# A first weight block fetched by two queues, weight conversions moved half a piece ahead, and two masks moved from DVE to ScalarE and GpSimd

## The chip, the cores and the metric

One core of a Trainium2 chip runs the kernel. The metric is the device time in microseconds of one execution. Engines are named as the profile names them: PE is TensorE, DVE VectorE, ACT ScalarE, POOL GpSimd, SP SyncE (here only an issuer of transfers); a q behind a name is the engine's instruction queue.

## What is computed

A gated linear attention over 768 steps for 4 batches and 8 heads of 48, and a feed-forward block on its output:

```python
for t in range(S):                       # S = 768, D = 48
    state = alpha[t][:, None] * state + outer(k[t], v[t])
    y[t] = q[t] @ state
x = y as (tokens 3072, 384)
h = x @ w_in                             # 384 x 1024
solu = h * softmax(h)
ln = (solu - mean) / sqrt(var + 1e-6) * g_ln
out = ln @ w_out                         # 1024 x 384
```

The weights w_in and w_out arrive as 64-bit floats, and the kernel turns them into 32-bit ones on the chip.

## The kernel before, in words

The 768 steps are cut into G = 6 groups of 128; one group holds 128 steps of all 4 batches, 512 tokens. Within a group the recurrence is done as matmuls: scaled keys and queries (running products of alpha, the scans of L220), scores of 128 x 128 per batch and head, a mask that keeps the causal half (`masked`, L290), then `read_values` (L343), which multiplies the masked scores with v and copies the result to x on ACT (L351). `keys_back` (L298) and `next_state` (L353) bring the state to the next group.

The feed-forward block then goes over the 1024 hidden columns in eight blocks f of 128. `up_mm` (L385) computes h for block f on PE: three matmuls, which stand as six records in the trace. `up_act` (L395) lets ACT make e = Exp(h) (L403), DVE the product u = h * e (L404) and ACT its Square (L405). `down` (L494) multiplies u with w_out. h has two banks in PSUM.

The order of the work is written out by hand, engine by engine, in program order: each engine executes its instructions in the order in which the code names them, and there is no scheduler that moves them. The group 0 part, L645 to L745, is the part that the change touches. It is also where the weights come in:

- `pieces` (L543) are eight: 0 to 3 are 256 columns each of w_in, 4 to 7 are 256 rows each of w_out.
- `fetch(i, slot, n)` (L552) issues on SP the transfers of n pieces from piece i on into raw space. For w_in that is 16 transfers: eight of 32 rows (4 KB a row, 128 KB) and eight of 16 rows (64 KB). `fetch(0, 3, 2)` (L662) brings pieces 0 and 1, `fetch(2, 1, 2)` (L663) pieces 2 and 3. Ahead of them SP issues alpha, k, q and v of group 0. In front of each transfer the issuing engine waits for the earlier transfer that used the same of eight semaphores.
- `bits(i, half)` (L585) converts a piece on DVE in five instructions: two in half 0 (L595, L598), three in half 1 (L603, L606, L607). `in_range(i)` (L575) lets ACT look for values out of range (L582, L583).
- `scaled` (L609) multiplies w_out rows with g_ln on ACT.

In the attention part of group 0, scores are in eight tiles: four (`a`, heads 0 to 3 of each batch) and four (`a_h`, `a_h`, `a_o`, `a_o`, heads 4 to 7 of batches 0 to 3). DVE masks all eight (L293). In the loop over f at L713 DVE does the product of f and then half a piece of conversion, `bits(2 + f // 2, f % 2)`, so that the four pieces 2 to 5 are spread over eight steps; bits(6) and bits(7) follow behind the loop. The loop also holds ACT work at fixed steps: in_range(2) at f = 1, copies of the ends of k and q at 2 and 3, in_range(3) at 3, in_range(4) at 5, scaled at 6 and 7.

Of the kernel before, what the change touches and what calls it, by code (L numbers as in the profile page):

```python
# [11 lines left out]
U32 = mybir.dt.uint32  # L12
I32 = mybir.dt.int32
AF = mybir.ActivationFunctionType
ALU = mybir.AluOpType
AX = mybir.AxisListType
P = 128
# [15 lines left out]
def fast_path(ctx, tc, q, k, v, alpha, moe_w_in, moe_w_out, moe_g_ln, out):  # L33
# [12 lines left out]
    nc = tc.nc  # L46
    B, H, S, D = q.shape
# [4 lines left out]
    NP = H // 2  # L52
# [26 lines left out]
    mask = const.tile([P, P], FP, name="mask")  # L79
    ones = const.tile([P, P], FP, name="ones")  # L80
# [8 lines left out]
    mean_sb = const.tile([P, DM], FP, name="mean_sb")  # L89
# [11 lines left out]
    qn = const.tile([P, H, TQ, D], FP, name="qn")  # L101
# [29 lines left out]
    sT = const.tile([P, B, H, P], FP, name="sT")  # L131
# [13 lines left out]
    def by_token(x):  # L145

        return x.rearrange("p h u d -> p (h u d)").rearrange("p (b h d) -> p b h d", b=B, h=H)

    def load_first(src, dst, g):
        t = slice(g * P, (g + 1) * P)  # L150
        for b in range(0, B, 2):
            nc.sync.dma_start(
                out=by_token(dst)[:, b : b + 2].rearrange("p b h d -> p (b h) d"),
                in_=src[b : b + 2, :, t].rearrange("b h p d -> p (b h) d"),
            )

    def ends_of(src, tag=None):

        ends = ring.tile([P, T4], FP, name=tag) if tag else two.tile([P, T4], FP, tag="two", name="ends")
        ends = ends.rearrange("p (b d) -> p b d", b=B)  # L160
        nc.scalar.copy(out=ends.rearrange("p b (h d) -> p b h d", h=H), in_=by_token(src)[:, :, :, E0:D])
        return ends
# [83 lines left out]
    def apart():  # L246
        for i in range(2):
            nc.scalar.mul(
                out=qv[:, H : 2 * H].rearrange("p (j i) t -> p j i t", i=2)[:, :, i], in_=qe, mul=parity[:, i : i + 1]
            )  # L250
# [19 lines left out]
    def quarter(b):  # L270
        return slice(32 * b, 32 * b + 32)

    def banks(name, shape, n=B):
        return [ps_a.tile([P] + shape, FP, tag=f"a{b}", name=f"{name}{b}") for b in range(n)]

    def scores(g, half, a=None):
        a = a or banks("a", [NP, P])
        for i in range(NP):
            h = half * NP + i
            for kb, qb in ((h, h), (H + h // 2, H + h)):  # L280
                for b in range(B):
                    nc.tensor.matmul(  # L282
                        a[b][:, i], lhsT=kT[quarter(b), kb], rhs=qv[quarter(b), qb], start=kb == h, stop=kb != h,
                        tile_position=(32 * b, 0), skip_group_check=True,
                    )
        masks[half] = a
# [3 lines left out]
    def masked(half, batches=range(B)):  # L290
        a = masks[half]
        for b in batches:
            nc.vector.tensor_tensor(  # L293
                out=sT[:, b, half * NP : half * NP + NP], in0=a[b], in1=mask[:, None, :].to_broadcast([P, NP, P]),
                op=ALU.mult,
            )
# [11 lines left out]
    parts = [(a, [(NP * a + r, first_of[r % 2]) for r in range(NP)]) for a in range(2)]  # L308
# [237 lines left out]
    def place(i):  # L546
        kind, f = pieces[i]
        return w_out[:, f : f + 2, 0:DM] if kind else w_in[:, :, f * P : f * P + 2 * P]

    raws = {}  # L550

    def fetch(i, slot, n=1):  # L552

        kind, f = pieces[i]
        w = n * F // (2 if kind else KC)
        raw = room[:, 1536 * slot : 1536 * (slot + n)].bitcast(U32).rearrange("p (c f w) -> p c f w", f=w, w=2)
        if kind:
            parts = [(slice(0, P), c, moe_w_out[(f + c) * P : (f + c + 1) * P, :]) for c in range(2)]
        else:
            rows = moe_w_in[:, f * P : f * P + w].rearrange("(h d) f -> h d f", d=D)  # L560
            parts = [(slice(E0 * r, E0 * r + E0), c, rows[NP * c + r, 0:E0]) for c in range(2) for r in range(NP)]
            parts += [(slice(E1 * h, E1 * h + E1), 2, rows[h, E0:D]) for h in range(H)]
        for rows, c, src in parts:
            if float64:
                nc.sync.dma_start(out=raw[rows, c].rearrange("p f w -> p (f w)"), in_=src.bitcast(U32))
            else:
                dst = w_out[rows, f + c, 0:DM] if kind else w_in[rows, c, f * P : f * P + w]
                nc.sync.dma_start(out=dst, in_=src)
        for m in range(n):
            raws[i + m] = raw[:, :, w // n * m : w // n * (m + 1)]  # L570

# [13 lines left out]
    def bits(i, part=None):  # L585
        if not float64:
            return
        lo, hi = raws[i][:, :, :, 0], raws[i][:, :, :, 1]
        if part != 1:
            made[i] = [  # L590
                two.tile([P, F], FP, tag="two", name=x).rearrange("p (c f) -> p c f", c=hi.shape[1])
                for x in ("top", "low")
            ]
            top = made[i][0].bitcast(U32)
            nc.vector.tensor_scalar(  # L595
                out=top, in0=hi, scalar1=3, scalar2=0x3FFFFFF8, op0=ALU.logical_shift_left, op1=ALU.bitwise_and
            )
            nc.vector.scalar_tensor_tensor(  # L598
                out=top, in0=hi, scalar=0xC0000000, in1=top, op0=ALU.bitwise_and, op1=ALU.bitwise_or
            )  # L600
        if part != 0:
            top, low = made.pop(i)
            nc.vector.tensor_scalar(  # L603
                out=low.bitcast(U32), in0=top.bitcast(U32), scalar1=0xFF800000, scalar2=None, op0=ALU.bitwise_and
            )
            nc.vector.scalar_tensor_tensor(out=low, in0=lo, scalar=2.0**-52, in1=low, op0=ALU.mult, op1=ALU.mult)  # L606
            nc.vector.tensor_tensor(out=place(i), in0=low, in1=top, op=ALU.add)  # L607
# [34 lines left out]
    def inline(x, name):  # L642
        return nc.inline_tensor(np.ascontiguousarray(x, np.float32), name=name).ap()

    load_first(alpha, an, 0)  # L645
    nc.scalar.dma_start(out=ident, in_=inline(np.eye(P), "ident_c"))
    nc.scalar.dma_start(out=mask, in_=inline(np.triu(np.ones((P, P))), "mask_c"))
    odd = np.arange(P) // E1 % 2
    nc.scalar.dma_start(out=parity, in_=inline(np.stack([1 - odd, odd], 1), "parity_c"))
# [9 lines left out]
        nc.gpsimd.memset(s, 0.0)  # L659
    nc.gpsimd.memset(state, 0.0)  # L660
    load_v_first(0)
    fetch(0, 3, 2)  # L662
    fetch(2, 1, 2)  # L663
    nc.vector.memset(ones, 1.0)
    nc.vector.memset(small_ones, 1.0 / 32)
    nc.vector.memset(mhalf, -0.5)
    nc.vector.memset(mone, -1.0)
# [7 lines left out]
    t = three("tp_a", [(ps_a, "a0"), (ps_a, "a1"), (ps_a, "a2")])  # L675
# [4 lines left out]
    t = three("tp_k", [(ps_a, "a3"), (ps_h, "h"), (ps_h, "h")])  # L680
# [7 lines left out]
    t = three("tp_q", [(ps_o, "o"), (ps_o, "o"), (ps_a, "a0")])  # L688
    turned(qn, ends_of(qn), t)
    for i in (2, 0, 1):  # L690
        if i == 1:
            scan_on(0, i)
        part = slice(NP * i, NP * i + NP)
        nc.vector.tensor_tensor(
            out=qe if i == 2 else qv[:, part], in0=t[i], in1=aT[:, part, 1:SW], op=ALU.mult
        )
        if i == 2:
            apart()
    scores(0, 0)
    t = [x.tile([P, NP, P], FP, tag=n, name="a_" + n) for x, n in ((ps_h, "h"), (ps_o, "o")) for _ in range(2)]  # L700
    scores(0, 1, t)
    read_begin()
    masked(0)
    masked(1)
    bits(0)
    read_values(0)
    gains()
# [3 lines left out]
    in_range(1)  # L711

    for f in range(FC):  # L713
        p = 2 + f // 2
        up_mm(0, f)
        if f == 4:
            array_sums(0, 0)
        up_act(0, f)
        bits(p, f % 2)
        if f == 0:  # L720
            next_state(0)
            fetch(4, 3)
            load_first(k, kn, 1)
            load_first(q, qn, 1)
            load(alpha, an, 1)
        elif f == 1:
            in_range(2)
        elif f == 2:
            ends_k = ends_of(kn, "e")
        elif f == 3:  # L730
            in_range(3)
            ends_q = ends_of(qn, "u2")
        elif f == 4:
            fetch(5, 1)
            fetch(6, 2)
        elif f == 5:
            in_range(4)
            fetch(7, 3)
            load_v(1)
        elif f == 6:  # L740
            scaled(4)
        elif f == 7:
            scaled(5)
    bits(6)
    tk = three("tp_k", [(ps_a, "a2"), (ps_a, "a3"), (ps_h, "h")])  # L745
    turned(kn, ends_k, tk)
    load(k, kn, 2)
# [129 lines left out]
    for g in range(1, G + 1):  # L877
# [10 lines left out]
        for s in range(FC):  # L888
# [17 lines left out]
            if step:  # L906
                n, half = step
# [17 lines left out]
    parts = [N * 3, G * 2, G * NB] + [len(pieces)] * 2  # L925
# [5 lines left out]
    def compare(out, x, bound, op):  # L931
# [6 lines left out]
        out=chunks[:, :, 2], in0=sums[:, :, 2], scalar=0.25, in1=sums[:, :, 3], op0=ALU.mult, op1=ALU.is_le  # L938
# [6 lines left out]
    else:  # L945
# [9 lines left out]
        out=bad, in0=all_ok[0:1, 0:1], scalar1=float(P * ends[-1]), scalar2=None, op0=ALU.is_lt  # L955
# [451 lines left out]
```

## Time and profile before

| what | value |
|---|---|
| four runs | 390.88, 391.44, 395.19, 395.36 us, median 393.31 |
| the profiled execution | 395.23 us, its span 393.2 us |
| busy, share of the span | PE 95%, PE weight loads 57%, DVE 64%, ACT 37%, POOL 32% |
| mean granted PE clock | 0.99 |
| first masks to last masks on DVE | 21.72 to 26.58 us |
| first conversion, bits(0) | starts at 28.61 us |
| first block h on PE | starts at 33.29 us |
| first product u on DVE | starts at 38.53 us |
| last conversion, bits(7) | ends at 73.12 us |
| POOL between its last copy of v and its next operation | 22.8 to 85.79 us |

The page gives busy time by engine and by fortieth of the span. The waits name, for each idle stretch of an engine, the instruction that ended it. The order of time lists each engine's instructions with their start and their duration in us; "x4" means that four were put together in one line, and the bracket holds the idle time ahead of it. Times in a line are start, then duration. An instruction's duration is a little longer than the distance to the next one, since they overlap at the ends.

### The profile page before, as it was taken

Reading aid. Unit: us, or ns where it says so; the run is one execution under the profiler, and the core shown is the slowest. Engines: PE = TensorE matmul, PEld = TensorE weight load, DVE = VectorE, ACT = ScalarE, POOL = GpSimd, SP = SyncE. Lnnn points to the kernel's source line nnn. Section 1 sums busy time; section 2 is a strip of 40 time slices with the busy share of each in tenths; the row PEclk is TensorE's granted clock in tenths of the full one; section 3 lists DMA queues with packets and bytes.
Section 4 is the critical chain, followed back from the end, with each engine's and each line's share of the span. In section 5 each row is a group of like instructions: output and inputs, shape, how many; then the busy total and the mean of one; then the engine's idle time right before and its main releaser. Section 6 shows DMA issues by size and latency. Waiting matters only on the chain. (4 is left out here: it accounts for less than half of the span.)

```text
span 393.2 us, 10613 instructions
## 1 busy us (share of the span) xinstructions
PE 371.7 (95%) x4661; PEld 224.0 (57%) x4661; DVE 251.6 (64%) x421; ACT 143.8 (37%) x252; POOL 124.7 (32%) x135
## 2 busy tenths in 40 slices
PE   8696999888899999999998999999999999999995
PEld 8683435455665456556555556556555575555552
DVE  0978788995898867694655694655895511444420
ACT  2625675645315425224252224253223231333100
POOL 4010000023032993337413337413535620333210
PEclk9998999998999999999999999999999999999999
DMA  9956979602367303643021634000600000000011
GB/s 187 187 162 174 233 210 177 140 0 72 74 160 103 82 3 83 85 99 101 22 62 44 88 95 102 22 2 23 82 20 22 22 23 2 20 21 21 22 42 48
DMA packets 86567, 30.79 MB, mean 78 GB/s; under 512 B 68072, under 2 KB 84720, under 8 KB 86512
## 3 DMA queue, kind: packets, MB, share of 16 engines
q1 hardware_dynamic: 85488, 29.11, 34.2%
q10 hardware_dynamic: 1024, 0.92, 0.7%
q8 instruction: 38, 0.62, 0.7%
q14 instruction: 17, 0.14, 0.1%
HBM read 25.30 MB, written 4.72 MB: 76 GB/s over the span
## 5 line engine op out<-in xcount | busy, mean ns | idle before, releaser
L389 PE MATMUL h<-x,w_in 128*128 128x512 f32 x288 | 133.9, 605 | 3.4 <-DVE g_col L619 3.3
L500 PE MATMUL o<-w_out,room 128*128 128x385 f32 x384 | 133.9, 492 | 1.0 <-DVE least L234 1.0
L500 PEld LDWEIGHTS o<-w_out,room 128*128 128x128 f32 x384 | 71.5, 190 | 57.5 <-issue 14.7
L389 PEld LDWEIGHTS h<-x,w_in 128*128 128x128 f32 x288 | 53.6, 191 | 63.0 <-issue 49.3
L404 DVE TENSOR_TENSOR room<-h,e 128x512 f32<-128x512 f32 x40 | 27.6, 690 | 83.0 <-ACT e L403 83.0
L403 ACT ACTIVATE e<-h 128x512 f32<-128x512 f32 x40 | 23.9, 598 | 103.7 <-PE h L389 103.7
L531 POOL TENSOR_TENSOR r<-sums,mhalf 128x1 f32<-128x1 f32 x20 | 14.3, 715 | 143.0 <-DVE sums L523 143.0
L420 POOL TENSOR_TENSOR p<-p,e 128x512 f32<-128x512 f32 x30 | 41.7, 1390 | 15.8 <-ACT e L403 15.7
L405 ACT ACTIVATE u<-room 128x512 f32<-128x512 f32 x40 | 25.2, 630 | 42.1 <-DVE room L404 42.1
L293 DVE TENSOR_TENSOR sT<-a,mask 128x512 f32<-128x512 f32 x44 | 27.2, 680 | 10.5 <-PE a L282 10.5
L282 PE MATMUL a<-qv,kT 32*128 32x128 f32 x704 | 27.6, 288 | 4.1 <-DVE least L234 1.7
L282 PEld LDWEIGHTS a<-qv,kT 32*128 32x128 f32 x704 | 24.1, 194 | 11.6 <-issue 4.4
L220 DVE TENSOR_TENSOR_SCAN hT<-aT,unit 128x516 f32<-128x516 f32 x18 | 23.1, 1340 | 8.6 <-ACT aT L678 8.6
L244 POOL TENSOR_TENSOR kT<-kT,hT 128x1024 f32<-128x1024 f32 (+1 forms) x8 | 13.3, 1678 | 44.4 <-DVE kT L195 44.4
L420 DVE TENSOR_TENSOR p<-p,u 128x512 f32<-128x512 f32 x30 | 23.1, 769 | 6.5 <-ACT u L405 6.5
L314 PE MATMUL y<-sT,vn 128*32 128x128 f32 x768 | 23.6, 274 | 2.6 <-issue 2.0
L314 PEld LDWEIGHTS y<-sT,vn 128*32 128x32 f32 x768 | 20.9, 110 | 4.8 <-issue 3.6
L220 DVE TENSOR_TENSOR_SCAN aT<-aT,seed 128x516 f32<-128x516 f32 x18 | 23.0, 1277 | 0.6
L212 ACT ACTIVATE sq<-an,mone 128x1536 uint8<-128x1536 f32 x12 | 18.8, 1570 | 0.2
L314 PE MATMUL y<-qv,state 32*32 32x128 f32 x960 | 16.8, 277 | 1.0 <-DVE sT L293 0.9
L314 PEld LDWEIGHTS y<-qv,state 32*32 32x32 f32 x960 | 12.1, 103 | 7.9 <-issue 4.8
L533 ACT ACTIVATE o_sb<-o,r 128x384 f32<-128x384 f32 x16 | 9.3, 580 | 18.8 <-POOL r L531 15.6
(142 smaller groups left out, 377.5 us busy)
## 6 DMA issues: line engine op xcount, KB each, us to landing
an<-in_alpha_dram SPq DMA_DIRECT2D x20, 192.0 KB, 3.7
out_dram<-o_sb SPq DMA_DIRECT2D x20, 192.0 KB, 1.9
room<-in_moe_w_out_dram SPq DMA_DIRECT2D x8, 384.0 KB, 4.0
kn<-in_k_dram SPq DMA_DIRECT2D x16, 192.0 KB, 4.1
qn<-in_q_dram SPq DMA_DIRECT2D x16, 192.0 KB, 3.9
vn<-in_v_dram SPq DMA_DIRECT2D x10, 256.0 KB, 3.9
room<-in_moe_w_in_dram SPq DMA_DIRECT2D x16, 128.0 KB, 3.6
kn<-in_k_dram SPq DMA_DIRECT2D x4, 384.0 KB, 5.9
```

The costliest lines, as they stand in the source:

```text
L212: nc.scalar.activation(out=sq, in_=x, func=AF.Relu, scale=sign, bias=mone, accum_out=over[:, g, i : i + 1])
L220: nc.vector.tensor_tensor_scan(out=o, data0=a, data1=s, initial=1.0, op0=ALU.mult, op1=ALU.add)
L282: nc.tensor.matmul(a[b][:, i], lhsT=kT[quarter(b), kb], rhs=qv[quarter(b), qb], start=kb == h, stop=kb != h, tile_position=(32 * b, 0), sk ...
L293: nc.vector.tensor_tensor(out=sT[:, b, half * NP : half * NP + NP], in0=a[b], in1=mask[:, None, :].to_broadcast([P, NP, P]), op=ALU.mult,)
L314: nc.tensor.matmul(y_bank(b)[quarter(r), a], lhsT=lhsT, rhs=rhs, start=(b, r) not in begun, stop=stop, tile_position=(row, 32 * r), skip_g ...
L389: nc.tensor.matmul(h, lhsT=w_in[:, a, f * P : (f + 1) * P], rhs=d["x"][:, a].rearrange("p b t -> p (b t)"), start=(a == 0), stop=(a == KC ...
L403: nc.scalar.activation(out=e, in_=h, func=AF.Exp)
L404: nc.vector.tensor_tensor(out=u, in0=h, in1=e, op=ALU.mult)
L405: nc.scalar.activation(out=u2, in_=u, func=AF.Square)
L420: eng.tensor_tensor(out=p, in0=d[0][i] if f == 1 else p, in1=d[f][i], op=ALU.add)
L500: nc.tensor.matmul(d["o"][:, 0 : DM + 1], lhsT=u_of(g, f)[:, b * P : b * P + P], rhs=w_out[:, f], start=(f == 0), stop=(f == FC - 1), skip ...
L531: nc.gpsimd.tensor_tensor(out=r, in0=s[:, 3:4], in1=mhalf, op=ALU.pow)
```

## The change

Five edits, all in the group 0 part:

- the memset of `ones` goes to the front, and ACT copies one column of it into `mean_sb` right behind its first transfer; the activation table is loaded there
- `fetch` can take a queue and a selection of its transfers: of the first w_in block SP issues the eight of 32 rows, and ACT the eight of 16 rows, behind `apart()`
- of the eight masks DVE does six; the tiles of batches 2 and 3 of the second half are copied from PSUM by ACT and multiplied with the mask by GpSimd
- in the loop `bits` runs half a piece ahead: the whole of bits(2) at f = 0, then one half in each step up to the first half of bits(6) at f = 7
- at f = 3 the two fetches that stood in step f = 4 are issued, ahead of the copy of q's ends

```diff
-    def fetch(i, slot, n=1):
+    def fetch(i, slot, n=1, queue=nc.sync, some=slice(None)):
...
-        for rows, c, src in parts:
+        for rows, c, src in parts[some]:
             if float64:
-                nc.sync.dma_start(out=raw[rows, c].rearrange("p f w -> p (f w)"), in_=src.bitcast(U32))
+                queue.dma_start(out=raw[rows, c].rearrange("p f w -> p (f w)"), in_=src.bitcast(U32))
...
     nc.scalar.dma_start(out=ident, in_=inline(np.eye(P), "ident_c"))
+    nc.vector.memset(ones, 1.0)
+    nc.scalar.copy(out=mean_sb[:, 0:1], in_=ones[:, 0:1])
...
-    fetch(0, 3, 2)
+    fetch(0, 3, 2, some=slice(0, H))
     fetch(2, 1, 2)
-    nc.vector.memset(ones, 1.0)
...
         if i == 2:
             apart()
+    fetch(0, 3, 2, nc.scalar, slice(H, 2 * H))
     scores(0, 0)
...
     masked(0)
-    masked(1)
+    masked(1, (0, 1))
+
+    for b in (2, 3):
+        x = sT[:, b, NP:H]
+        nc.scalar.copy(out=x, in_=t[b])
+        nc.gpsimd.tensor_tensor(out=x, in0=x, in1=mask[:, None, :].to_broadcast([P, NP, P]), op=ALU.mult)
     bits(0)
     read_values(0)
...
     for f in range(FC):
-        p = 2 + f // 2
         up_mm(0, f)
         if f == 4:
             array_sums(0, 0)
         up_act(0, f)
-        bits(p, f % 2)
+
+        for half in (0, 1) if f == 0 else (f + 1,):
+            bits(2 + half // 2, half % 2)
...
         elif f == 3:
             in_range(3)
-            ends_q = ends_of(qn, "u2")
-        elif f == 4:
             fetch(5, 1)
             fetch(6, 2)
+            ends_q = ends_of(qn, "u2")
...
-    bits(6)
+    bits(6, 1)
```

## The prediction

> **What bounds the kernel now.** I read the page first (busy time by slice, granted clock), then the waits of the first 70 us, then the order of time on each engine from 18 to 92 us.
>
> ```profile
> PE   8696999888899999999998999999999999999995
> DVE  0978788995898867694655694655895511444420
> PEclk9998999998999999999999999999999999999999
> ```
>
> One digit is 9.83 us. TensorE is full from slice 11 (108 us) to the end, so nothing behind that can give time: the change can only bring that full stretch forward or push it back. Ahead of it DVE stands at 8 and 9 while PE has gaps.
>
> ```profile
> DVE top L595 <- DMA room<-in_moe_w_in_dram: 2.0, 1, 2.0
> PE h L389 <- DVE g_col L619: 3.3, 1, 3.3
> DVE room L404 <- ACT sT L403: 5.5, 6, 1.6
> ```
>
> Before DVE starts the first conversion it waits 2.0 us for the raw w_in; PE then waits 3.3 us for that conversion; and in the first feed-forward loop DVE waits 5.5 us for ScalarE's Exp.
>
> ```profile
> 25.31 1.27 DVE L293 TENSOR_TENSOR sT<-a_o,mask 128x512 f32<-128x512 f32 x2
> 28.61 0.95 DVE L595 TENSOR_SCALAR top<-room 128x768 uint32<-128x768 uint32 x1 [2.03 <-DMA room<-in_moe_w_in_dram]
> ...
> 38.53 0.69 DVE L404 TENSOR_TENSOR room<-h,sT 128x512 f32<-128x512 f32 x1 [0.81 <-ACT sT L403]
> ...
> 42.71 0.69 DVE L404 TENSOR_TENSOR room<-h,sT 128x512 f32<-128x512 f32 x1 [1.64 <-ACT sT L403]
> ...
> 73.12 0.44 DVE L460 STREAM_TRANSPOSE cols<-rows 128x256 f32<-128x256 f32 x1
> ```
>
> The two last masks end at 26.58, bits(0) begins at 28.61, and the last conversion, bits(7), ends at 73.12. From 62.6 to 91.5 DVE shows no wait (28.86 us busy of the 30 from 62 to 92), while PE waits for it at 72.6, 85.4 and 89.6 (the last 1.5 us). So **the yardstick is when DVE ends bits(7)**: what it gains or loses there reaches the full stretch of PE one for one.
>
> ```profile
> 28.41 1.53 PE L301 MATMUL tp<-ident,kT 128*128 128x128 f32 x12
> 33.29 4.51 PE L389 MATMUL h<-x,w_in 128*128 128x512 f32 x6 [3.35 <-DVE g_col L619]
> 37.73 1.55 PE L364 MATMUL kv<-vn,kg 128*32 128x48 f32 x96
> 39.20 10.85 PE L389 MATMUL h<-x,w_in 128*128 128x512 f32 x24
> ```
>
> The first block h of six records takes 4.51 us; the next 24 take 10.85, that is 2.71 for six. The clock was granted at 0.50 from 33.7 to 37.1, after the 3.35 us gap, and again from 91.7 to 95.1.
>
> ```profile
> 18.89 1.33 ACT L248 ACTIVATE qv<-qe,parity 128x512 f32<-128x512 f32 x2 [3.18 <-DVE qe L694]
> ...
> 30.54 0.93 ACT L582 ACTIVATE sq<-room 128x768 f32<-128x768 f32 x1
> ...
> 37.83 0.60 ACT L403 ACTIVATE sT<-h 128x512 f32<-128x512 f32 x1 [3.31 <-PE h L389]
> ```
>
> ```profile
> 13.39 21.00 SPq L565 DMA_DIRECT2D room<-in_moe_w_in_dram  x32
> ```
>
> ACT is free from 20.2 to 25.8, runs in_range(0) and (1) from 30.5 to 34.5, then waits for h. SP issues 32 w_in transfers in 21 us; the sixteenth, the last of the first block, is issued at 25.7 and landed at 28.4.
>
> **The change part by part.**
>
> *Two queues.* SP keeps the eight 128 KB transfers of block 0 and then goes on to block 2; ACT issues the eight of 64 KB after apart(), from 20.25. An issue takes 0.42 us, one per 0.46. On ACT the fifth to eighth each wait for the landing of the one four before (they share a semaphore). With the row's median of 2.9 us from issue to landing for 64 KB, they go at 20.25, 20.7, 21.2, 21.65, 23.15, 23.6, 24.1, 24.55, ACT is free at 25.0 and the block has landed at 27.45. SP's fifth now waits for v, landed at 20.8 (before it went at 19.42); its eighth goes at about 22.6 and lands at 26.2 (3.6, the median of 128 KB). So bits(0) starts at 27.5 rather than 28.6. Bounds: with the shortest landing in these rows, 2.3, it is 26.4; with 3.6 on ACT as well, 28.9. I take 27.5, since 64 KB has its own row. Block 2 on SP has six issues behind ACT's last four landings; at 0.46 each it ends issuing at about 31.5 and lands at 34.5, against 36.9 before and a need at 37: nothing.
>
> *Table load and a one-column copy at the start of ACT.* The load of 1.28 us at 6.71 goes to 1.1 us. The copy it stood ahead of ended at 8.63 and was needed by PE at 9.56; tp_a is set by the warm-up matmuls that end at 7.86. Nothing; mask and parity are issued 1.5 us later and are needed at 21.7 and 18.9 (landed by 5.0 before).
>
> *Two masks.* DVE loses two of 0.63, ending at 25.38, and then waits for w_in until 27.5: worth nothing alone. New path: ACT copies 0.58 (0.53 apart) from 25.05 to 26.16; GpSimd products of 1.27 (the 128x512 row of L420) from 25.75 to 27.0 and to 28.3. read_values needs the third and fourth: PE's blocks of 0.87 end at 27.95 and 29.2 (before 28.3), keys_back at 30.85 (29.94). ACT's kg copies end near 31.4 (30.66) and in_range(0), (1) with their 4.0 us at 35.4 (34.5). All this is one chain, **products, y, x, kg, in_range, first Exp**, and it has no slack left: the first Exp can't start before 35.4.
>
> *First block h.* bits(0) takes 4.44, so h starts at 32.05 (33.29); PE has waited 1.2 us and not 3.35, so I take the full clock, 2.71, and h ends at 34.8. Exp(0) starts at 35.4, set by ACT. DVE holds bits(1) until 27.5+4.44+0.1+4.6 = 36.6, so the first product u is at 36.6 instead of 38.53: **1.9 earlier**.
>
> *Conversions half a piece ahead.* The number of conversions is the same. In the loop, between the product of f and that of f+1, ACT does Square 0.6, perhaps in_range 1.9 or another copy 0.5, and Exp 0.6; DVE does one half: the first 1.9 (w_in) or 1.5 (w_out), the second 2.45. Before, the long half stood against the in_range steps; now it is the short one. Followed row by row from 36.6: u1 at 41.6 (42.71 before; the whole of bits(2) stands ahead of it), in_range(2) to 44.8, u2 at 45.4 (46.46) with DVE idle 1.4; u3 48.5 (48.92); u4 52.8 (53.23), idle 2.25; u5 55.9 (55.34); u6 59.7 (59.09), idle 1.7; u7 62.8 (61.97). DVE's idle time in the loop is 5.3 against 5.5. Then one half less is left: bits(7) ends at 71.4 instead of 73.12. Transfers needed half a piece sooner: piece 5 lands at about 55, needed at 56.5; that is the tightest.
>
> **Sum: -1.1 for the start, -0.6 net from idle time: 1.7.** The profiled execution took 395.23 (span 393.2), so such an execution takes 393.5. The four runs before are 390.88, 391.44, 395.19 and 395.36: two groups, median 393.31; the profile is of the upper one. Its two stretches at half clock cost 4.51-2.71 = 1.8, and about 1.4 at 91.7 (62 score records in 3.27, where 64 take 2.07 later): 3.2 of the 4.0 between the groups. I estimate that the lower group doesn't have them. In it the first u was at 37.7 already and by the same walk bits(7) at 71.4: the change gives nothing there, 391.2. Halfway between 391.2 and 393.5 is **392.4**, which I predict.
>
> *The skill against the rows.* The trace shows 0.50 for 3.4 us after a gap of 3.35 us, and 1.00 through a gap of 1.7 us at 18 us. The Trainium skill ("TensorE: Matmul & The Clock Gate", Part 1) says that the gate looks at free-running windows of about 3.4 us: the same gap may or may not throttle, by chance of phase. By it the new 1.2 us gap rarely would, which is what the rows gave me.
> The Trainium skill ("GPSIMD Engine Reference", 2.1) says that the first call of newly loaded code pays about 6 us. This speaks against the change: two pool-configuration instructions stand at 22.7 in the trace, and the next GpSimd product came 63 us later, so no row here shows such a price; by the page the products would start at about 28.7 and the sum would be 0.7 slower instead of 1.7 faster.
>
> **Rivals.**
>
> *The GpSimd products are late (slower).* Place: the first product, 25.75. Each us that it starts later moves y, x, kg, in_range and the first Exp by one; past 0.3 us nothing hides it. It decides at 28.0: then bits(7) is back at 73.1. For it: the configuration at 22.7 must be done, and its only later use was covered by 63 us. Against: the first product after it (0.56) took no longer than the later ones (0.54 to 0.57). If it takes what a transfer takes here from issue to landing, 1.8 to 10.4 us, the start is between 25.75 and 33.1; with the 5.9 of the 384 KB loads of k it is 28.65, +0.7, or 395.9 in the upper group and 393.7 in the lower (2.5 over 391.2): 394.8. At 33.1 it is +5.1, 400.
>
> *The block does not come sooner.* ACT's transfers share 16 engines with SP's; bits(0) at 28.9 gives 1.4 us less than my sum: -0.3, 394.9 and 392.6, 393.8. For it: the first block's landings of 64 KB reached 3.4 and 4.0. Against: from 23 to 29 the DMA engines moved 90 to 158 GB/s where 240 are seen at 29.
>
> *More than the sum.* Both half-clock stretches vanish: 393.5-1.4 = 392.1 in the upper group, 391.2 in the lower, 391.6.
>
> **How the numbers follow.** Forecast 0.48, late products 0.27, block not sooner 0.12, both stretches gone 0.10, others 0.03. Within 1% (389.4 to 397.2), about what a measurement of this kernel can tell from no change, lie the first, third and fourth, and most of the second: 0.82. Slower by over 1% needs the products to start after about 31: 0.09. Faster by over 1% is in no walk; 0.09 for a median that falls wholly in a lower group or for idle time that I left standing. Range 390.4 to 396.4, from the lower group less 0.8 for w_in at its earliest bound, to late products in the upper group; the forecast's own is 391.0 to 393.6.
>
> **What would show it.** bits(0) near 27.5; no 0.50 clock at 34; GpSimd products at 25.75 and 27.0; first u at 36.6; DVE idle 1.4, 2.25 and 1.7 ahead of u2, u4 and u6; bits(7) ending at 71.4. It is wrong if the products start after 28, if h starts after 33.3, or if DVE waits for piece 5 at 56.5.

## The result, and the profile after

The changed kernel takes 395.91 us (median of 52 runs, 392.18 to 399.28) against 393.8 us for the kernel before (median of 78 runs, 390.53 to 398.88). Its ratio to before is 1.0044, with a 95% interval of 1.0029 to 1.006. That is about 1.7 us slower: small, but the interval excludes no difference. (The ratio leaves out the slowest runs of both kernels, so it is not the 2.1 us between the medians.) The forecast was 392.4, 0.9 us faster than the four runs of before that it had; 395.91 lies within its range of 390.4 to 396.4, but on the slower side of before.

The profiled execution after took 397.39 us, span 395.6, against 395.23 and 393.2 before: +2.2 and +2.4. Its page has these lines for busy time by slice (one digit is 9.89 us) and for granted clock:

```profile
PE   8697999988989999999998999999999999999995
DVE  0958878996996878595566594655795521444420
PEclk9988999999899999999999999999999999999999
```

The picture is the one of before: PE is full from slice 11 on, so the difference has to be found ahead of it. The waits from 15 to 70 us (who waited for what: us in total, times, longest) already name the place:

```profile
DVE room L404 <- ACT sT L403: 5.8, 4, 2.2
ACT sT L710 <- DMA room<-in_moe_w_in_dram: 5.8, 1, 5.8
POOL sT L711 <- ACT sT L710: 4.0, 1, 4.0
...
DVE top L595 <- DMA room<-in_moe_w_in_dram: 2.9, 1, 2.9
...
PE h L389 <- DVE g_col L619: 2.3, 1, 2.3
```

DVE's wait for the raw w_in has grown from 2.0 to 2.9 us. ACT has a new wait of 5.8 us, spent between its own transfers, and behind it GpSimd waits 4.0 us. The order of time on DVE (start, us, instruction, in brackets the idle time before it):

```profile
25.44 1.27 DVE L293 TENSOR_TENSOR sT<-a_h,mask 128x512 f32<-128x512 f32 x2
29.64 0.95 DVE L595 TENSOR_SCALAR top<-room 128x768 uint32<-128x768 uint32 x1 [2.93 <-DMA room<-in_moe_w_in_dram]
...
39.47 0.69 DVE L404 TENSOR_TENSOR room<-h,sT 128x512 f32<-128x512 f32 x1 [0.73 <-ACT sT L403]
...
48.26 0.69 DVE L404 TENSOR_TENSOR room<-h,sT 128x512 f32<-128x512 f32 x1 [1.20 <-ACT sT L403]
...
55.70 0.69 DVE L404 TENSOR_TENSOR room<-h,sT 128x512 f32<-128x512 f32 x1 [2.23 <-ACT sT L403]
...
62.49 0.69 DVE L404 TENSOR_TENSOR room<-h,sT 128x512 f32<-128x512 f32 x1 [1.59 <-ACT sT L403]
...
74.25 0.44 DVE L460 STREAM_TRANSPOSE cols<-rows 128x256 f32<-128x256 f32 x1
```

The last mask on DVE ends at 26.71, bits(0) starts at 29.64 where it started at 28.61, and bits(7) ends at 74.25 where it ended at 73.12 (read, as in the prediction, from the start of what follows it; the table further on uses its recorded end, 0.08 later). The conversions have lost 1.0 us at their start and 1.1 us at their end. ACT and GpSimd at the head of it:

```profile
19.12 0.80 ACTq L565 DMA_DIRECT2D room<-in_moe_w_in_dram  x2
...
19.94 6.26 ACTq L565 DMA_DIRECT2D room<-in_moe_w_in_dram  x6
26.25 1.08 ACT L710 COPY sT<-a_o 128x512 f32<-128x512 f32 x2 [5.80 <-DMA room<-in_moe_w_in_dram]
```

```profile
26.91 2.52 POOL L711 TENSOR_TENSOR sT<-sT,mask 128x512 f32<-128x512 f32 x2 [3.97 <-ACT sT L710]
```

ACT needs until 26.25 to issue its eight transfers, because the fifth to eighth each wait for a landing, and can't start the two copies before that. PE:

```profile
30.43 1.53 PE L301 MATMUL tp<-ident,kT 128*128 128x128 f32 x12
34.31 4.43 PE L389 MATMUL h<-x,w_in 128*128 128x512 f32 x6 [2.34 <-DVE g_col L619]
...
92.33 2.06 PE L282 MATMUL a<-qv,kT 32*128 32x128 f32 x62 [1.48 <-DVE qv L788]
94.31 2.86 PE L500 MATMUL o<-w_out,room 128*128 128x385 f32 x8
...
102.25 4.55 PE L500 MATMUL o<-w_out,room 128*128 128x385 f32 x8
```

The gap ahead of the first h is 2.34 us, the clock is granted at 0.50 from 34.15 to 37.57, and h takes 4.43 us, nearly the 4.51 of before. The scores of group 1 start at 92.33, where before has:

```profile
91.10 3.27 PE L282 MATMUL a<-qv,kT 32*128 32x128 f32 x62 [1.48 <-DVE sums L518]
```

The 1.1 us from bits(7) has arrived there, plus 0.1. What comes behind is chance of one execution: before, a half-clock stretch lay on these scores (3.27 us), here it lies on the matmuls at 102 (4.55 us, where the eight at 94.31 took 2.86).

The transfers issued from 19 to 30 us (KB each, median us from issue to landing), before and then after:

```profile
room<-in_moe_w_in_dram SPq DMA_DIRECT2D x12, 128.0 KB, 3.5
room<-in_moe_w_in_dram SPq DMA_DIRECT2D x8, 64.0 KB, 2.8
```

```profile
room<-in_moe_w_in_dram SPq DMA_DIRECT2D x11, 128.0 KB, 4.1
room<-in_moe_w_in_dram ACTq DMA_DIRECT2D x8, 64.0 KB, 4.5
```

The 64 KB transfers that had landed after 2.8 us on SP's queue take 4.5 on ACT's, beside SP's 128 KB ones, which went from 3.5 to 4.1. The last of the block landed at 28.43 before and at 29.36 after.

### The profile page after: what moved, and what is told of

It is laid out like the page before. It is cut to its first block, busy times and chain, and to the rows that moved or that the text cites. A ratio compares the mean times of both kernels' runs of the same rounds, so it can differ in the third digit from the quotient of the medians.

```text
span 395.6 us, 10619 instructions
## 1 busy us (share of the span) xinstructions
PE 374.1 (95%) x4661; PEld 225.0 (57%) x4661; DVE 250.6 (63%) x419; ACT 144.7 (37%) x255; POOL 128.0 (32%) x137
## 3 DMA queue, kind: packets, MB, share of 16 engines
q1 hardware_dynamic: 85232, 28.58, 33.7%
## 5 line engine op out<-in xcount | busy, mean ns | idle before, releaser
L404 DVE TENSOR_TENSOR room<-h,e 128x512 f32<-128x512 f32 x40 | 27.7, 693 | 85.5 <-ACT e L403 85.5
L293 DVE TENSOR_TENSOR sT<-a,mask 128x512 f32<-128x512 f32 x44 | 27.3, 680 | 9.9 <-PE a L282 9.9
L282 PE MATMUL a<-qv,kT 32*128 32x128 f32 x704 | 27.4, 288 | 4.6 <-DVE least L234 2.2
```

Source lines behind the costliest of these rows:

```text
L282: nc.tensor.matmul(a[b][:, i], lhsT=kT[quarter(b), kb], rhs=qv[quarter(b), qb], start=kb == h, stop=kb != h, tile_position=(32 * b, 0), sk ...
L293: nc.vector.tensor_tensor(out=sT[:, b, half * NP : half * NP + NP], in0=a[b], in1=mask[:, None, :].to_broadcast([P, NP, P]), op=ALU.mult,)
L404: nc.vector.tensor_tensor(out=u, in0=h, in1=e, op=ALU.mult)
```

## The experiments

My theory after the result: **the two queues land the block about 1 us later, and that is the whole loss**. Rivals: the conversions half a piece ahead cost time further on; the masks' way over ACT and GpSimd delays x; the half clock at 34 us is what costs, and would cost however the block came. All ratios below are to the kernel before, with their 95% intervals; times at points of the kernel come from one profiled execution each. Code cuts are marked with three dots.

### One part alone, or all but one

e1, the two queues with the early table load (whose lines and the new arguments of `fetch` are as in the change):

```diff
-    fetch(0, 3, 2)
+    fetch(0, 3, 2, some=slice(0, H))
...
+    fetch(0, 3, 2, nc.scalar, slice(H, 2 * H))
     scores(0, 0)
```

> Only the two queues and the early table load; masks on DVE, conversions as before. Theory Q (the two queues bring the first w_in block later, and that is the whole loss): bits(0) starts at about 29.6 us against 28.6 before, the sixteen transfers of the block landing 3.3 to 7 us after their issue, bits(7) ends about 1.0 later at 74.1, ratio 1.003 to 1.005. Theory P (the loss is the chain through ScalarE copies and GpSimd products): without it the first Exp isn't held up, ratio 0.997 to 1.001. Theory H (the loss is the later products u): ratio 1.000 to 1.002.

Measured: 1.0067 [1.0031, 1.0103]; bits(0) at 28.97, bits(7) ends at 73.7. Below are ACT's last six transfers, which still hold it for 5.16 us, and the copy of x that is its next work:

```profile
20.34 5.16 ACTq L565 DMA_DIRECT2D room<-in_moe_w_in_dram  x6
27.14 0.48 ACT L351 COPY x<-y 128x384 f32<-128x384 f32 x1 [6.57 <-DMA room<-in_moe_w_in_dram]
```

This part alone is slower: its interval excludes no difference and overlaps that of the whole change, with nothing moved in the loop and no mask on GpSimd. That ACT is held so long is not what sets the time: in the profiles of all five kernels that issue eight of the transfers on ACT (after, e1, e5, e8, e11), ACT still waits 1.6 to 5.0 us for h before its first Exp, and h starts within 0.2 us of the end of bits(0).

e2, the conversions half a piece ahead (with the two fetches moved to f = 3):

```diff
+        for half in (0, 1) if f == 0 else (f + 1,):
+            bits(2 + half // 2, half % 2)
...
```

> Only the conversions half a piece ahead (with the two fetches moved to f = 3). Theory Q: bits(0) as before at 28.6; product u of f = 7 about 2.3 us later than before, near 64.3, but bits(7) ends at 72.9 to 73.2 as before, since the order of the work on DVE doesn't change its sum; ratio 0.998 to 1.001. Theory H: PE reaches the first down two us later and doesn't make it up; ratio 1.003 to 1.006.

Measured: 0.998 [0.9944, 1.0017]. It costs nothing that can be measured.

e3, the two masks:

```diff
-    masked(1)
+    masked(1, (0, 1))
+    for b in (2, 3):
...
+        nc.scalar.copy(out=x, in_=t[b])
+        nc.gpsimd.tensor_tensor(out=x, in0=x, in1=mask[:, None, :].to_broadcast([P, NP, P]), op=ALU.mult)
```

> Only the two masks moved to ScalarE copies and GpSimd products; ScalarE issues no transfers. Theory Q: the copies start when the scores are done, near 24 us, the products end by 27, the fourth y is at most 0.5 us later than before and the first Exp is set by h; ratio 0.998 to 1.002. Theory P: the products are late whatever ScalarE does, the fourth y ends after 29 and the first product u is later than 38.5; ratio 1.002 to 1.005.

Measured: 1.0008 [0.9972, 1.0043], nothing either. Its GpSimd:

```profile
24.34 2.52 POOL L709 TENSOR_TENSOR sT<-sT,mask 128x512 f32<-128x512 f32 x2 [1.75 <-ACT sT L708]
```

The product starts 1.8 us after the pool configuration (at 22.54 in the trace), and it waits for ACT's copy and for nothing else. x is not late either: ACT's kg copies, which stand behind it, end at 30.3, against 30.7 before.

e4, the change without the two queues (the whole block on SP):

```diff
-    fetch(0, 3, 2, some=slice(0, H))
+    fetch(0, 3, 2)
...
-    fetch(0, 3, 2, nc.scalar, slice(H, 2 * H))
```

> The changed kernel with the first w_in block on SP alone (16 transfers as before, masks on ScalarE and GpSimd, conversions half a piece ahead, table load early). Theory Q: bits(0) at 28.6, bits(7) ends at 72.9 to 73.2, ratio 0.998 to 1.001, so about 0.4% better than the changed kernel. Theories P and H: the loss stays, ratio 1.003 to 1.006.

Measured: 1.0025 [0.9986, 1.0063]; span 391.2 in the profiled execution. In that execution the block happened to land early, bits(0) started at 27.34, and DVE then ran as I had forecast for the whole change:

```profile
27.34 0.96 DVE L595 TENSOR_SCALAR top<-room 128x768 uint32<-128x768 uint32 x1 [0.58 <-DMA room<-in_moe_w_in_dram]
36.60 0.68 DVE L404 TENSOR_TENSOR room<-h,sT 128x512 f32<-128x512 f32 x1
41.64 0.68 DVE L404 TENSOR_TENSOR room<-h,sT 128x512 f32<-128x512 f32 x1
45.37 0.69 DVE L404 TENSOR_TENSOR room<-h,sT 128x512 f32<-128x512 f32 x1 [1.20 <-ACT sT L403]
...
62.64 0.69 DVE L404 TENSOR_TENSOR room<-h,sT 128x512 f32<-128x512 f32 x1
```

```profile
32.25 2.81 PE L389 MATMUL h<-x,w_in 128*128 128x512 f32 x6 [0.94 <-DVE g_col L619]
```

First u at 36.60, u1 at 41.64, u7 at 62.64, bits(7) ending at 71.4, h at full clock behind a gap of 0.94 us. The walk was right for a block that is there at 27.4. Over all runs the kernel is not faster: the early block was that execution's luck. The interval holds both what was expected if the queues are the loss and what was expected if they are not, so e4 alone decides nothing.

e5, the change without the half-ahead conversions (queues, table load and masks); e8, the two queues without the table load:

> The changed kernel with the conversions in the loop as before (two queues, table load and the two masks stay). Theory Q (the late first block is the loss): bits(0) at 28.9 to 29.7, bits(7) ends 0.5 to 1.1 later than before, ratio 1.003 to 1.007, as with the queues alone. Theory H (the later products u are the loss): ratio 0.998 to 1.001.

> Only the two queues, without the early table load and memset. Theory Q: as with the table load, ratio 1.003 to 1.009, bits(0) at 28.9 to 29.7. If the early table load were the cause of the loss seen with both: ratio 0.998 to 1.002 and bits(0) at 28.6 or sooner.

Measured: 1.0008 [0.9969, 1.0046] with bits(0) at 29.40 and bits(7) at 73.97; and 1.0037 [0.9994, 1.008] with bits(0) at 29.95 and bits(7) at 74.66. In e8 bits(0) is late without the table load too, which speaks against the load as the cause. e5's ratio lies below the 1.003 that the theory asked for, and alone would allow no loss at all.

### Fewer and larger transfers

e6 asks whether the number of issues is what delays the block: three transfers of 128 rows instead of 16 for each block. e7 adds the half-ahead conversions.

```diff
-            parts = [(slice(E0 * r, E0 * r + E0), c, rows[NP * c + r, 0:E0]) for c in range(2) for r in range(NP)]
-            parts += [(slice(E1 * h, E1 * h + E1), 2, rows[h, E0:D]) for h in range(H)]
+            parts = [(slice(0, P), c, rows[NP * c : NP * c + NP, 0:E0]) for c in range(2)]
+            parts += [(slice(0, P), 2, rows[:, E0:D])]
```

> The kernel before, with each w_in block on SP in 3 transfers of 128 rows (512 KB) and not 16 of 32 and 16 rows. Theory Q says that the block's landing sets the start of the conversions, and that the many issues and the waits between them set the landing: issued by about 18, the block lands near 26.5, bits(0) starts at 26.6 right behind the masks, bits(7) ends 1.5 to 2 earlier, ratio 0.993 to 0.997. Rival: the landing is set by what the DMA engines move, not by issues: bits(0) stays at 28 to 28.6, ratio 0.999 to 1.002.

> As the merged one, and the conversions half a piece ahead. Theory Q: bits(0) at 26.6, first product u near 35.8 to 36.6 set by DVE, DVE idle 1.4, 2.2 and 1.7 ahead of u2, u4 and u6, so no better than the merged one alone: ratio 0.993 to 0.998. Theory H: 0.3% worse than the merged one alone.

Measured: 1.0229 [1.0182, 1.0275] and 1.0324 [1.0259, 1.0388]. In e6:

```profile
35.11 0.95 DVE L595 TENSOR_SCALAR top<-room 128x768 uint32<-128x768 uint32 x1 [8.95 <-DMA room<-in_moe_w_in_dram]
```

The expectation, an earlier block, was missed: it is 6.5 us later than before. In the records, 5 and 9 separate signals report the end of such transfers, where the others have 16, and the last two of the six issues took 7.95 and 5.33 us. From 19 to 27 us the DMA share was 0.41, at 96 GB/s (0.61 and 170 before). So it seems that these transfers were carried by a few of the 16 engines. The Trainium skill ("DMA: Bandwidth & Descriptors", "Why a DMA increments its semaphore by 16 and not by 1") states that the slowest dimension of the transfer sets how many engines take part; the four and eight heads that stand outermost here would give four and eight, with one more signal for the rest, which agrees with the 5 and 9. The experiment therefore tells nothing about the number of issues, but it shows what late blocks cost: 6.5 us later at bits(0), 8.8 later at bits(7) (81.99), 2.3% of the time. The second block is late as well there, DVE waits another 4.08 us for it at 49.65, so this is not the price of the first alone. And e7 shows when half-ahead conversions cost: 0.3 us sooner at bits(0) than e6, but 1.6 later at bits(7).

### The half clock

Dummy matmuls of 128 columns (up to 16, two records each) behind `keys_back(0)` fill PE's gap ahead of the first h. e9 is before with 16 of them, e10 adds the half-ahead conversions, e11 is the whole change with 12, e12 is e4 with 14.

```diff
     keys_back(0)
+    warm(16)
     in_range(0)
```

> The kernel before with 16 dummy 128x128 matmuls on ones behind keys_back of group 0, that fill PE's gap ahead of the first block h (3 us at full clock by the rate of the warm-up at the start). Theory C (the half clock in the first block h costs 1.8 us, and that cost reaches the end): the clock stays at 1.00 there, h takes 2.7, first product u at 37.7, bits(7) ends at 71.4, ratio 0.994 to 0.998. Rival: the dummies only move the half clock elsewhere or the first product is set by something else: ratio 0.999 to 1.002.

> As e9, and the conversions half a piece ahead, nothing else. If the half ahead costs nothing (as the prediction had it): bits(7) ends as in e9, ratio as there. Theory H2 (with h at full clock the longer conversion ahead of u1 and the short halves against in_range leave DVE idle 5 us instead of 4): u0 37.7, u1 42.7, u7 64, bits(7) ends at 72.5, about 1.1 later than e9; ratio 0.997 to 1.001.

> The changed kernel with 12 dummy matmuls behind keys_back of group 0. Theory C: bits(0) at 29.0 to 29.7 as in the changed kernel, h at full clock, first product u at 38.3 to 38.8 set by bits(1), bits(7) ends near 73.3 and not 74.3; ratio 0.999 to 1.003.

> The changed kernel with the first w_in block on SP alone and 14 dummy matmuls behind keys_back. Theory Q plus C: bits(0) at 27.3 to 28.6, first product u at 36.6 to 37.7, bits(7) ends at 71.4 to 72.5, ratio 0.996 to 1.000; better than e11 by about 0.9 us, what the two queues cost. If the queues cost nothing, the same as e11.

Measured: 0.9979 [0.9945, 1.0012], 1.0004 [0.9978, 1.0031], 1.0045 [1.0005, 1.0084] and 0.9999 [0.9968, 1.003]. In e9:

```profile
31.07 3.74 PE L445 MATMUL warm<-ones 128*128 128x128 f32 x32
34.64 2.74 PE L389 MATMUL h<-x,w_in 128*128 128x512 f32 x6
```

The first h runs at full clock (2.74 and 2.81 us) in the profiles of all four, but the dummies took more than the 3.0 us that I had estimated: in e9 bits(0) was done at 32.36, and h started at 34.64. First u at 38.12 against 38.53: 0.4 us. So e9 says little about what the full clock is worth. The changed kernel keeps its loss with the full clock in the first h (e11, 1.0045, though its interval comes near 1), so the half clock there does not explain it. e11 and e12 differ in the queues and in two dummies: 1.0045 and 0.9999, in the direction of the theory, but their intervals overlap. e10 against e9 is the half-ahead conversions at an equal first u (38.13 and 38.12): u7 is 2.6 us later (64.13 against 61.56), bits(7) 0.1 later (72.91 against 72.80). The later u's push the first `down` from 63.96 to 66.51, and PE makes that up before group 1 (scores at 90.92 and 90.72).

### Why the block is late

e13 is e1 without the fetch of block 2 (its transfers follow those of the first block on SP); e14 is before without it.

```diff
-    fetch(2, 1, 2)
+    raws[2], raws[3] = raws[0], raws[1]
```

> The two queues alone (as e1), and the second w_in block isn't fetched at all: pieces 2 and 3 convert the raw data of pieces 0 and 1, so only the start up to bits(0) is read. If SP's transfers of block 2, which go out before ScalarE's last ones, are what holds the first block up: it lands by 27.5, as the prediction had it. If it is the waits of one transfer for another on the eight shared semaphores and the long landings of two queues: bits(0) stays at 28.7 to 29.9.

> The kernel before, and the second w_in block isn't fetched (as e13). On one queue the block is complete before block 2 starts, so both theories expect bits(0) as before, at 27.3 to 28.6.

One execution each. In e13 DVE got the block no sooner:

```profile
29.69 0.95 DVE L595 TENSOR_SCALAR top<-room 128x768 uint32<-128x768 uint32 x1 [1.76 <-issue]
```

So in this execution ACT's transfers were slow without block 2; the last of the first block landed at 29.51. e14 also showed 29.70, against 28.61 before: on one queue too an execution can be that late. There the sixteenth issue took 1.91 us instead of 0.42, and the last four landed 3.5 to 4.0 us after their issue. A single start of bits(0) is thus no proof, and I go by groups below.

e15 leaves twelve transfers on SP and gives ACT only the last four of 64 KB, without the table load; e16 adds 14 dummies.

```diff
-    fetch(0, 3, 2)
+    fetch(0, 3, 2, some=slice(0, 12))
...
+    fetch(0, 3, 2, nc.scalar, slice(12, 16))
     scores(0, 0)
```

> Two queues with only the last four transfers of 64 KB on ScalarE, twelve on SP, no early table load; all else as before. ScalarE's transfers then wait for at most one other, and ScalarE is free at 21.6. If the waits on one another are the cause: the block lands by 27.5, bits(0) at 26.7 to 27.6, ratio 0.996 to 0.999. If any second queue makes it late: bits(0) at 28.7 or later, ratio 1.002 to 1.005.

> As e15, with 14 dummy matmuls behind keys_back of group 0. If e15 brings the block by 27.5: h at full clock from about 32.2, first product u 36.8, bits(7) ends near 71.3, ratio 0.994 to 0.998, better than both kernels. Else as e9, or worse by what the block is late.

Measured: 1.0024 [0.9991, 1.0057] and 1.0003 [0.9967, 1.0039]. The block landed at 27.9 and 27.7, bits(0) started at 28.11 and 27.88, right behind DVE's masks. The transfers of e15 from 19 to 30 us:

```profile
room<-in_moe_w_in_dram SPq DMA_DIRECT2D x11, 128.0 KB, 3.0
room<-in_moe_w_in_dram ACTq DMA_DIRECT2D x4, 64.0 KB, 3.8
room<-in_moe_w_in_dram SPq DMA_DIRECT2D x4, 64.0 KB, 2.8
```

While both queues have work, ACT's 64 KB take 3.8 us; SP's later ones, alone, take 2.8 again. ACT's four have landed at 25.0, in good time; with eight, the second four start only from landings like these. The block came between the two expectations (by 27.5, or bits(0) at 28.7 and later), so these two kernels don't decide between them; no gain of time came of them.

### All together

| kernels | first w_in block | bits(0) starts | bits(7) ends | ratio to before |
|---|---|---|---|---|
| after, e1, e5, e8, e11 | half on ACT's queue | 28.97 to 29.95, mean 29.6 | 73.7 to 74.7, mean 74.1 | e1, e5, e8, e11: 1.0040 ± 0.0020 |
| before, e2, e3, e4, e9, e10, e12 | SP's queue | 27.3 to 29.6, mean 28.4 | 71.4 to 74.9, mean 73.1 | e2 to e12: 0.9999 ± 0.0013 |
| e15, e16 | four transfers on ACT's queue | 28.1, 27.9 | 71.0, 72.4 | 1.0024 and 1.0003, each ± 0.0035 |

The ratios in the last column are means weighted by the intervals. The intervals of one set of runs share its runs of before, so the ± are a little too small. The kernels with half the block on ACT's queue lose 0.40% against before, those with the block on SP's queue nothing; the difference, 0.41% or 1.6 us ± 0.9, is the measured loss of the change within its interval, and the 1.0 us between the means at bits(7) is of that size, though the kernels of each group scatter by 1.0 and 3.5 us there. The landing of the block's last transfer tells the groups apart better, since the masks don't move it: 28.70 to 29.67 us, mean 29.3, with half the block on ACT, and 27.16 to 29.44, mean 28.2, on SP alone. In the first group it is ACT's half that lands last in every profile. The part that costs is the two queues; this rests on e1 and on the groups, since other single kernels lie on both sides (e5, e4). The masks and the half-ahead conversions neither cost nor bring anything that can be measured here, the late blocks of e7 aside.

No kernel is clearly faster than before: e9, with 0.9979 [0.9945, 1.0012], is not clear of before.

How little one execution tells here is seen from what lies behind the yardstick. The span less the end of bits(7) should be the same everywhere, and goes from 317.7 (e16) to 322.6 us (e6). It follows the mean granted clock: 317.7 to 318.4 in the three executions with 0.995 to 0.998, 319.7 to 321.3 from 0.984 to 0.994, and 321.5 to 322.6 in the four below. A microsecond won at bits(7) drowns in that in any single pair of profiles.

## Why the prediction was right or wrong

- **The bound and the yardstick: right.** Group 1's scores start 17.9 to 18.1 us after the recorded end of bits(7) in every profile, from e4 (71.4) to e7 (83.6). This holds within one execution; what a microsecond there is worth over runs is less sure (e15 ended bits(7) 2.2 us sooner than before in its profile, and was not faster over its runs).
- **Two queues: wrong, and this is the step that failed.** The prediction said: "With the row's median of 2.9 us from issue to landing for 64 KB, they go at 20.25, 20.7, 21.2, 21.65, 23.15, 23.6, 24.1, 24.55, ACT is free at 25.0 and the block has landed at 27.45." That median was taken from transfers that had one queue behind them. The first four were issued sooner than I said (19.12 to 20.60), but they landed 3.2 to 5.3 us after issue, so that the four that wait for a landing went at 22.38, 22.82, 24.58 and 25.89, and the block had landed at 29.36. SP's own last one, due at 22.6, went at 23.52 and landed at 28.58. bits(0) started 2.1 us later than forecast and later than the latest bound I gave, 28.9: with 3.6 us from issue to landing that bound was too short as well. The records show how the landings hold the issues: the block's sixteen transfers use the same eight semaphores on two queues as on one (ACT's fourth, at 20.60, went when SP's first had landed, at 20.58). So a second queue doesn't let more of them be under way at once.
- **The rate: half right, and no help.** I spoke against my own rival with "from 23 to 29 the DMA engines moved 90 to 158 GB/s where 240 are seen at 29". That stretch did fill, but the one ahead of it moved less. The windows from 19 to 27 and from 23 to 29 us (length, busy us of PE, PEld, DVE, ACT and GpSimd, granted clock, DMA share, GB/s), before and then after:

```profile
19.00:27.00 8.00, 6.83 (x216) 6.29 (x220) 7.41 (x13) 2.06 (x4) 1.95 (x5) 1.00 0.61 170
23.00:29.00 6.00, 5.43 (x170) 4.83 (x163) 3.97 (x7) 1.91 (x4) 0.00 (x0) 1.00 0.42 126
```

```profile
19.00:27.00 8.00, 6.67 (x168) 6.31 (x172) 6.53 (x12) 2.09 (x4) 2.70 (x5) 0.79 0.78 162
23.00:29.00 6.00, 5.36 (x167) 4.71 (x164) 3.68 (x6) 1.94 (x4) 2.09 (x2) 0.92 0.74 162
```

  From 23 to 29 us the five kernels with eight transfers on ACT moved 162 to 189 GB/s (mean 177), the seven with the whole block on SP 112 to 174 (mean 143). From 19 to 23 it was the other way: 170 to 202 (mean 188) and 197 to 222 (mean 213). And SP sent transfers of block 2 from 25.53 on, ahead of ACT's last of block 0 (25.89). From 19 to 27 the five moved 183 on the mean and the seven 170, 8% more. The DMA share adds up the times of packets (from 13 to 19 us before it is 1.06), so 0.78 instead of 0.61 says that the packets took more time, not that the engines did more. A packet of 4 KB took 224 ns on the mean of 19 to 27 us before and 300 after; over the two groups 249 and 275. The Trainium skill ("DMA: Bandwidth & Descriptors", "Rules for kernel authors") says that spreading transfers over the issuing engines doesn't help bandwidth, as all share the 16 DMA engines, and that it saves only issue time. These runs agree nearly: 8% of rate, and no sooner block. The prediction gave the shared engines only a rival at 0.12; the rule spoke against this change.
- **ACT's time: missed.** With the same 2.9 us for a landing, ACT was to be free at 25.0. It was held until 26.25, which moved the copies by 1.2 us and the products by as much. It cost nothing further on: ACT waited 2.21 us for h before the first Exp.
- **Masks: right in price, late in place.** Products of 1.26 us each, from 26.91 instead of 25.75. The rival "late products" had the right sign, but not its cause: they were late because ACT was. The 6 us that the Trainium skill ("GPSIMD Engine Reference", 2.1) names for the first call of newly loaded code were not seen: in e3 the product started 1.8 us after the configuration, on the copy's heels. Whether that code was newly loaded, no row shows.
- **First h: wrong, following from the block.** The gap was 2.34 us instead of 1.2, and the clock went to half for 3.4 us. Where the gap was small (e4, 0.94) h took 2.81 us against a forecast of 2.71. That is 1.6 us in one execution, but over runs no gain was seen (e9, e12). The prediction weighed the phase of a free-running window; the clock's records show such a window: see the last section.
- **Half ahead: right.** DVE's idle time ahead of u2, u4 and u6 was 1.20, 2.23 and 1.59 us (forecast 1.4, 2.25, 1.7). From the first u to the end of bits(7) passed 34.8 us, as forecast, against 34.6 before: the conversion that is taken out of the end had been put in front of u1.
- **The sum.** The forecast had the first u at 36.6; it came at 39.47, 2.87 later, 2.14 from the block and 0.73 from the slower way to u. From there everything ran as written. Of the terms, -1.1 for the start became +1.0, and -0.6 from idle time became +0.1, since the wait ahead of the first u, which was to vanish (0.81 before), was still 0.73.
- **The two groups of runs: wrong.** Four runs looked like 391.2 and 395.3; 78 runs spread over 390.5 to 398.9 without a gap. The half clock is no switch between two groups either: its stretches last 3.41 us, or two or three times that (6.83 in e2, 10.24 in e6), and their number and places change (33.7 and 91.7 before; 20.5, 34.2 and 102.4 after; 20.7 and 99.2 in e4; 35.0 alone in e8; none in e11). Taking the mean of two supposed groups hid that the gain was to be set against all runs.
- **The rival "the block does not come sooner"** had the right mechanism. It deserved more than 0.12, and a bound that let the block come later than before.

What stays open: why a packet takes longer when two queues feed the DMA engines. e13, one execution, speaks against block 2's transfers as the cause; whether it is the change from one queue to the other, or the two parts of the block that are written at once, was not tried.

## What to carry to other kernels

Don't price a transfer on a second queue by its latency on the first: where the engines already serve one queue's backlog, expect each transfer to take longer, and little more to be moved. An engine whose transfers wait for the landing of earlier ones is held as long as they are, so count the landing, not the issue, against what stands behind it. When single executions scatter by more than the step you are after, set a median against a median, and judge a part by several kernels that have it.

## What the runs showed of the hardware that was not expected

- On a second queue 64 KB took 4.5 us from issue to landing instead of 2.8 (median of 19 to 30 us; 3.9 to 4.6 in the five kernels with eight of them on ACT, 2.3 to 3.4 in the seven without), while the rate from 19 to 27 us hardly changed (170 and 162 GB/s; means of the groups 170 and 183).
- Three large transfers with four or eight heads outermost were much slower than 16 small ones: 96 GB/s in place of 170, and issues that took 5.3 and 8.0 us.
- The clock changes on a fixed grid of 3.41 us. Within a profile every complete stretch at one clock is a whole number of these steps (before: 27.31, 3.41, 54.61, 3.41 and 296.96 us, which are 8, 1, 16, 1 and 87), and the grid lies elsewhere in each execution. This is the free-running window of about 3.4 us of which the Trainium skill speaks ("TensorE: Matmul & The Clock Gate", Part 1); it has the half clock follow an idle window. Here a partly idle one was enough. Before 60 us, a window at full clock in which PE was busy up to 1.48 of 3.41 us (e5, 16.97 to 20.38) was followed by the half clock, with one exception at 1.47 (e8, 28.16 to 31.58); from 1.61 on (e14, 16.13 to 19.54) none was.
- The length of PE's gap splits the same cases. Ahead of the first scores, near 19 us, nine of the 18 profiles have a gap of 1.93 to 2.45 us, and in all nine the clock goes to half at about 20.5; the other nine have 1.48 to 1.85, and it stays at full. Ahead of the first h, gaps of 0.65 (e11, behind its dummies), 0.94 (e4) and 1.49 us (e15) left it at full, and those of 2.34 us (after) and more all brought the half clock. Gaps of 2 us were enough, then.
- Further on neither tells the cases apart: before, the clock also went to half at 91.7 us behind a window with 1.94 us of PE and a gap of 1.48 us; in e11 it stayed at full behind one with 1.93 us and the same gap. After, it went to half at 102.4 us behind a gap of 0.85. What decides there was not tried.
